# A retention block and two mixture-of-experts layers: rows of one step asked for once, scatters given out one per round, and a block of zero rows written behind other loads

## The chip, the cores and the metric

The kernel runs on one core of a Trainium2 chip. The metric is device microseconds of one execution. Five instruction streams run beside each other and wait for one another through semaphores: TensorE (PE, with its weight loads shown as PEld), VectorE (DVE), ScalarE (ACT), GpSimd (POOL) and SyncE (SP). SP computes nothing here; it issues the plain transfers. POOL issues the indirect ones (scatters of rows to places that a list of indices names).

## What is computed

The program is three stages in a row, all in float32:

```
# stage 1, for 4 batches x 8 heads, 576 positions, head size 64
scores = q @ k.T / sqrt(64)
ret    = scores * where(i >= j, gamma_h ** (i - j), 0)
x      = (ret @ v), heads side by side          # 2304 tokens x 512

# stage 2, "layer 1": 8 experts, capacity 576 rows each
e, g   = argmax(x @ w_gate), its softmax value
y[n]   = g * (relu(x[n] @ w1[e]) @ w2[e])       # 512 -> 1024 -> 512, by the token's expert

# stage 3, "layer 2": the same with other weights, only for tokens with y @ w_skip > 0
out[n] = y[n] + g2 * (relu(y[n] @ w1b[e2]) @ w2b[e2])     (else out[n] = y[n])
```

## The kernel before

**Attention.** A function `round_(u)` runs for u = 1 to 20 (`round_(0)` comes first). There are 20 units: 4 batches times 5, where four units are pairs of heads over the first 512 positions and the fifth is a tail with the last 64 positions of all heads. A round transposes the keys and queries of unit u + 1 (tiles `Tk`, `Tq`, line 187), multiplies by the states of unit u - 1 (`O`, lines 236 and 240), makes the scores of unit u (`S`, line 204), multiplies those of unit u - 1 by its values (line 246), makes the state of unit u + 1 (`kv`, line 216) and then asks for unit u + 5 (`load`). The scaled queries and values (`qp`, `vh`, function `prep`, lines 165 to 171) are made by POOL. Loads are kept in four buffers, so unit u + 4's loads wait for the buffers of unit u.

Between its parts a round has three places (`slot`) at which it takes one piece of work from a list `g.bg`. The pieces of a batch of tokens (`tokens_out(g, b)`) are: `logits`, `choose`, the rows (transposes `xps`, line 601), `step`, which computes the index of each row, and `put`. A `put` scatters T tiles of 128 rows (4 for even b, 5 for odd b) into the table `xs1` in memory: one indirect transfer for each tile, line 467. The list is `[logits, choose, rows.., step, rows.., put]` and starts for batch 0 in round 5, for batch 1 in round 11, for batch 2 in round 15; batch 3 follows after the attention.

The table of an expert's rows must hold zeros where no row is written. `clear(1)` does that for `xs1` (lines 1235 and 1238): 252 x 8 pieces of 32 bytes and 100 x 8 rows of 2080 bytes. It is issued by SP right behind the loads of unit 5. `clear(2)` does it for the table `xs2` of layer 2, late in the attention.

**Order.** In the attention the order of PE's work is written out by hand (`manual_schedule`); that of POOL, DVE, ACT and SP is chosen by the compiler's scheduler from the program's order and its own estimate of when each instruction is ready. In the layers only POOL's order is written by hand. Dependencies on the tables `xs1` and `xs2` are kept for the whole table: a read of rows waits for every scatter that stands ahead of it in the program, a scatter for every read ahead of it; scatters do not wait for each other.

**Layers.** Each layer has 9 steps (`pos` 0 to 8). A step takes one expert's rows, at most `CAPS[lay][pos]` of them (layer 2: 176, 324, 32, 240, ...), and that expert's weights in 4 units of 1 MB (`load_unit`, lines 678 and 679, five buffers). With more than 192 rows, the weights of a unit and the rows are split into a high and a low part: ACT makes `hi` (line 695), DVE `lo` (line 696), and a product is three matmuls. `gather(pos)` asks for a step's rows: four transfers of `xb` (line 649), one or two of `rows` (lines 663 and 665). `transposes` turns `xb` on DVE (line 722); with more than 192 rows ACT casts the result (`x_1h`, line 724) and DVE makes the rest (`x_1l`, line 725). `s1` is the first product of a step (`h`, lines 749, 754 to 756), `s2` the second (`y`, lines 814, 817 to 819). The step is cut in eight parts f = 0 to 7, two for each unit; `s1` runs one part ahead of `s2`. At f = 7 a step also runs `s1` part 0 of the next step. After a step, `post1` or `post2` turn the result (`yr`, line 845) and scatter it (line 467 into `xs2`, line 895 into the output).

**The line that asks twice.** In `Layer.run`, f counts the parts and u = base + 4 pos + f // 2 the units. Layer 2's first unit is 36 = 4 * NST:

```
if f == (0 if u == 4 * NST else 4) and (nx is not self or pos == 0):
    nx.gather(np_)
```

In layer 2's step 0, u is 36 at f = 0 and 1, 37 at f = 2 and 3, and 38 at f = 4 and 5. So the condition holds at f = 0 (u is 36) and at f = 4 as well (u is 38, and f is 4): the rows of layer 2's step 1 are asked for twice, into two sets of tiles, and what follows uses the second.

Of the kernel before, what the change touches and what calls it, by code (L numbers as in the profile page):

```python
# [29 lines left out]
NST = 9  # L30
# [16 lines left out]
LA = 3  # L47
# [58 lines left out]
def attention(g, hooks):  # L106
# [14 lines left out]
    def load(u):  # L121
        s = st[u] = K()
        b, p = s.b, s.p = u // 5, u % 5
        if tail(u):
            s.raw = g.ld.tile([128, 3, 2, 2, DH], F32, tag="t", name=f"t{b}", bufs=2)
            for i, x in enumerate((k, q, v)):
                for j in range(2):
                    nc.sync.dma_start(out=s.raw[64 * j:64 * j + 64, i].rearrange("p a h d -> p (a h) d"),
                                      in_=x[b, 4 * j:4 * j + 4, 512:576].rearrange("h p d -> p h d"))
            return  # L130
        hs = slice(2 * p, 2 * p + 2)
        s.q = g.ld.tile([128, 2, 4, DH], F32, tag="q", name=f"q{u}")
        s.k = g.ld.tile([128, 4, 2, DH], F32, tag="k", name=f"k{u}")
        s.v = g.ld.tile([128, 4, 2, DH], F32, tag="v", name=f"v{u}")
        dq = lambda: nc.sync.dma_start(out=s.q, in_=q[b, hs, 0:512].rearrange("h (p r) d -> p h r d", r=4))

        def pair(x, d):
            for hh in range(2):
                nc.sync.dma_start(out=d[:, :, hh], in_=x[b, 2 * p + hh, 0:512].rearrange("(t p) d -> p t d", p=128))

        part = lambda c0, c1: nc.sync.dma_start(out=g.tab[:, c0:c1], in_=g.ia["tab"][:, c0:c1])
        if u:
            dq()
            pair(k, s.k)
        else:
            pair(k, s.k)
            part(0, TAB0)
            dq()
        pair(v, s.v)
        if u == 0:  # L150
            part(TAB0, TAB1)
        elif u == 2:
            part(TAB1, g.tab.shape[1])
            g.small_loads()
        elif u == 5:
            g.clear(1)

    def prep(u):
# [113 lines left out]
    def round_(u):  # L272
        if u:
            slot()
        if u + 1 < NU:
            if u:
                prep(u + 1)
            transposes(u + 1, 0)
            if u:
                slot()  # L280
            transposes(u + 1, 1)
        if u:
            inter(u - 1)
            slot()
        if u < NU:
            scores(u)
        if u:
            pv(u - 1)
        if u + 1 < NU and not tail(u + 1):
            state(u + 1)  # L290
        if u + ahead < NU:
            load(u + ahead)
        if u:
            g.bg += hooks.get(u - 1, [])

# [273 lines left out]
def tokens_out(g, b):  # L569

    nc = g.nc
    n0 = 9 * (b // 2) + (4 if b % 2 else 0)
    T = 5 if b % 2 else 4
    s = K()

    def logits():
        s.l4 = g.rt1.tile([128, 640], F32, tag="l4", name=f"l4_{b}", bufs=1)
        logits4(g, g.xT[b], g.wg1, [512] if T == 4 else [320, 320], s.l4, f"L4_{b}_")

    def choose():  # L580
        L = g.rt1.tile([128, T, NL], F32, tag="L1", name=f"L1_{b}")
        token_logits(g, s.l4, T, L, f"Lt{b}_")
        s.xr = g.xr.tile([128, T, RW], F32, tag="xr", name=f"xr{b}")
        nc.gpsimd.tensor_copy(s.xr[:, :, TOK], g.tid1[:, n0:n0 + T])
        nc.gpsimd.memset(s.xr[:, :, VAL + 1:], 0.0)
        s.gen = g.r1.add(n0, T, L, f"r{b}", s.xr, late=b > 1)
        next(s.gen)

    def step():
        next(s.gen, None)  # L590

    def put():
        for t in range(T):
            g.r1.put(n0 + t, s.xr[:, t])
        g.r1.note(n0, T, s.xr)

    def row(t):
        n = n0 + t
        ps = misc(g, f"xps{n}")
        for c in range(4):  # L600
            nc.tensor.transpose(ps[:, 128 * c:128 * c + 128], g.xT[b][:, c, 128 * t:128 * t + 128], g.ident)
        nc.scalar.copy(stored(s.xr[:, t, 0:D]), natural(ps))

    rows = [lambda t=t: row(t) for t in range(T)]
    if b == 3:
        return [logits, choose] + rows, lambda: (step(), put())
    if b == 1:
        return [logits, choose, rows[0], rows[1], g.r1.pick_first, rows[2], step, rows[3], rows[4], put]
    return [logits, choose, rows[0], rows[1], None, rows[2], step, rows[3], put]


def ncap(u):
# [86 lines left out]
class Layer:  # L699
# [154 lines left out]
    def run(self, hooks, inner={}):  # L854
        g, lay = self.g, self.lay
        base = 4 * NST * (lay - 1)
        for pos in range(NST):
            for f in range(8):
                u = base + 4 * pos + f // 2
                if f % 2 == 0:  # L860
                    load_units(g, u + (LA if (lay, pos) < (1, 3) else LA2 - 1 if u == 4 * NST else LA2))
                    convert_unit(g, u + 1)
                    if self.small(pos) and f in (0, 4):
                        convert_unit(g, base + 4 * pos + 4 + f // 4)
                nx, np_ = (self, pos + 1) if pos < NST - 1 else (self.next, 0)
                if nx is not None:
                    if f == (0 if u == 4 * NST else 4) and (nx is not self or pos == 0):
                        nx.gather(np_)
                    for p in self.fetched(pos, f):
                        self.gather(p)  # L870
                    if nx is not self or pos == 0:
                        if f == 6:
                            nx.transposes(np_, [0, 1])
                            nx.transposes(np_, [2, 3])
                    elif f in (2, 4):
                        nx.transposes(np_, [f - 2, f - 1])
                for i in range(f + 1, f + 2 + (4 if self.small(pos) else self.token_major(pos))):
                    if i < 8:
                        self.s1(pos, i)
                    elif nx is not None and i < 9 + self.token_major(pos) and f > 4:  # L880
                        nx.s1(np_, i - 8)
                if f == 7 and nx is not None and nx.small(np_):
                    nx.s1(np_, 2)
                self.s2(pos, f)
                if (pos, f) in inner:
                    inner[pos, f]()
            self.evac(pos)
            self.post(pos)
            if pos in hooks:
                hooks[pos]()  # L890
# [284 lines left out]
def build(nc, tc, ia, oa, off, stage=99):  # L1175
    g = K()
    g.nc, g.tc, g.ia, g.oa = nc, tc, ia, oa
    g.wts, g.reg, g.xT = {}, {}, {}
    g.bg, g.scat = [], []
    with ExitStack() as ctx:  # L1180
        cp = g.cp = ctx.enter_context(tc.tile_pool(name="cp", bufs=1))
        dr = ctx.enter_context(tc.tile_pool(name="dr", bufs=1, space=DRAM))
# [65 lines left out]
        with ExitStack() as ac:  # L1248
            g.xb = ac.enter_context(tc.tile_pool(name="ge", bufs=1))
            g.ld = ac.enter_context(tc.tile_pool(name="ld", bufs=4))  # L1250
            g.wk = ac.enter_context(tc.tile_pool(name="wk", bufs=2))
            g.xt = ac.enter_context(tc.tile_pool(name="xt", bufs=2))
            ap = ac.enter_context(tc.tile_pool(name="ap", bufs=1))
            g.psT = ac.enter_context(tc.tile_pool(name="psT", bufs=1, space=PSUM))
            g.psS = ac.enter_context(tc.tile_pool(name="psS", bufs=2, space=PSUM))
            g.psO = ac.enter_context(tc.tile_pool(name="psO", bufs=1, space=PSUM))
            g.misc = ac.enter_context(tc.tile_pool(name="psX", bufs=2, space=PSUM))
            g.xtail = ap.tile([128, 4, DH], F32, name="xtail")
            e = Layer(g, 1, None)
            g.st0 = e.st  # L1260

            def loads():
                for u in range(LA):
                    load_unit(g, u)

            g.st3 = [ap.tile([128, 3, 128], F32, name=f"st3_{i}") for i in range(2)]
            g.st4 = [ap.tile([128, 4, 128], F32, name=f"st4_{i}") for i in range(2)]
            for x in g.st3 + g.st4:
                nc.gpsimd.memset(x, 0.0)
            attention(g, {  # L1270
                2: [small_prep],
                3: tokens_out(g, 0),
                9: tokens_out(g, 1) + [loads],
                13: tokens_out(g, 2) + [lambda: e.gather(0)],
                16: [lambda: clear(2)] + [lambda c=c: e.transposes(0, [c, c + 1]) for c in (0, 2)],
            })
            thunks, g.step3 = tokens_out(g, 3)
            with tc.manual_schedule(engines={mybir.EngineType.PE}):
                for fn in g.bg + thunks:
                    fn()  # L1280
        g.rt = mc.enter_context(tc.tile_pool(name="rt2", bufs=1))
        g.xb = mc.enter_context(tc.tile_pool(name="xb", bufs=3))
# [32 lines left out]
```

## Time and profile before

| | us |
|---|---|
| runs | 582.13 median of 3 (580.64 to 586.38) |
| the profiled execution, as a run | 578.59 |
| its span, from the first to the last instruction | 576.7 |
| PE's last product of the attention | 121 |
| PE's first product of layer 1's step 1 | 145 |
| PE's first product of layer 2's step 0 | 363 |
| PE's first product of layer 2's step 1 | 407 |

The page of the profile, its first two parts:

```
span 576.7 us, 12343 instructions
## 1 busy us (share of the span) xinstructions
PE 522.2 (91%) x4437; PEld 489.1 (85%) x4437; DVE 289.3 (50%) x881; ACT 218.9 (38%) x417; POOL 147.5 (26%) x225
## 2 busy tenths in 40 slices
PE   6959898999999999999999999980799599999994
DMA  8778889777999657575857555099597965879920
```

One digit is a slice of 14.4 us, in tenths of busy time. PE is busy in nine tenths of the span, so what is left to win is in the few slices with a lower digit: those of the first 40 us, and 28 to 32 (390 to 475 us).

### The profile page before, as it was taken

How to read it: one execution, taken by the hardware profiler on the slowest of the kernel's cores; microseconds unless marked ns; L12 is line 12 of the kernel's file. 1: busy time of each engine (PE TensorE's matmuls, PEld its weight loads, DVE VectorE, ACT ScalarE, POOL GpSimd, SP SyncE). 2: the span in 40 equal slices, each digit the busy share in tenths (PEclk: the TensorE clock that was granted, in tenths of full speed). 3: DMA queues.
4: the chain of work that ended last, by engine and by line, in shares of the span. 5: the costliest groups of instructions: out<-in, count | busy, mean ns of one | idle time of the engine just before them, and what ended most of it. 6: DMA issues, size and time to landing. Idle time of an engine off the chain costs nothing.

```text
span 576.7 us, 12343 instructions
## 1 busy us (share of the span) xinstructions
PE 522.2 (91%) x4437; PEld 489.1 (85%) x4437; DVE 289.3 (50%) x881; ACT 218.9 (38%) x417; POOL 147.5 (26%) x225
## 2 busy tenths in 40 slices
PE   6959898999999999999999999980799599999994
PEld 5949786979899999999999999980798489999994
DVE  4726594732467576766677765531446332211211
ACT  2224352441355464756566564321234131111110
POOL 4324736504304050414241505121002101101111
PEclk7889998999999999999999999995799799999998
DMA  8778889777999657575857555099597965879920
GB/s 194 150 196 197 243 207 320 247 235 240 291 316 291 203 176 204 173 203 160 218 178 201 181 182 155 13 258 271 142 291 197 368 198 176 256 251 296 301 83 26
DMA packets 140654, 122.35 MB, mean 212 GB/s; under 512 B 54995, under 2 KB 114131, under 8 KB 140583
## 3 DMA queue, kind: packets, MB, share of 16 engines
q1 hardware_dynamic: 134711, 108.73, 67.2%
q0 software_dynamic: 5872, 12.74, 5.9%
q8 instruction: 37, 0.61, 0.4%
q14 instruction: 34, 0.28, 0.2%
HBM read 103.21 MB, written 23.09 MB: 219 GB/s over the span
## 4 chain that ended last, share of the span: by engine, by line
PE 50%; issue 32%; DMA 6%; POOL 5%; SPq 3%; DVE 2%; ACT 1%; POOLq 0%; ACTq 0%; DVEq 0%
PE h L756 5%; PE h L755 5%; PE y L817 5%; PE h L754 5%; PE y L819 5%; PE y L818 5%; POOL out L895 3%; PE S L204 3%; DMA k<-k 2%; PE O L246 2%; DMA xs<-xr,idx 2%; PE h L749 2%; PE y L814 2%; PE Tk L187 2%; DMA r<-w1a 2%
## 5 line engine op out<-in xcount | busy, mean ns | idle before, releaser
L696 DVE TENSOR_TENSOR lo<-r,hi 128x1024 fp32r<-128x1024 f32 x72 | 87.9, 1224 | 56.3 <-ACT hi L695 54.3
L695 ACT CAST hi<-r 128x1024 fp32r<-128x1024 f32 x72 | 75.4, 1048 | 45.4 <-PE y L818 18.3
L814 PE MATMUL y<-hh,r 128*128 128x176 f32 (+4 forms) x512 | 81.8, 303 | 0.2 <-ACT hh L751 0.2
L817 PE MATMUL y<-hh,hi 128*128 128x316 f32 (+7 forms) x256 | 76.4, 300 | 0.0
L819 PE MATMUL y<-hh,lo 128*128 128x316 f32 (+7 forms) x256 | 76.0, 297 | 0.0
L818 PE MATMUL y<-hl,hi 128*128 128x316 f32 (+7 forms) x256 | 75.8, 297 | 0.0
L814 PEld LDWEIGHTS y<-hh,r 128*128 128x128 f32 x512 | 74.3, 190 | 0.5 <-ACT hh L751 0.4
L751 ACT ACTIVATE hh<-h 128x176 f32<-128x176 f32 (+4 forms) x64 | 19.6, 307 | 112.4 <-PE h L749 112.4
L895 POOL DMA_INDIRECT out<-o,oi x17 | 16.4, 968 | 165.8 <-DVE o L965 163.0
L759 ACT ACTIVATE hh<-h 128x316 fp32r<-128x316 f32 (+8 forms) x72 | 29.1, 404 | 75.9 <-PE h L756 75.8
L818 PEld LDWEIGHTS y<-hl,hi 128*128 128x128 f32 x256 | 48.3, 189 | 0.0
L819 PEld LDWEIGHTS y<-hh,lo 128*128 128x128 f32 x256 | 48.2, 188 | 0.0
L817 PEld LDWEIGHTS y<-hh,hi 128*128 128x128 f32 x256 | 48.1, 188 | 0.1
L760 DVE SCALAR_TENSOR_TENSOR hl<-h,hh 128x316 fp32r<-128x316 f32 (+8 forms) x72 | 32.2, 448 | 31.4 <-ACT hh L759 31.3
L833 DVE COPY yt<-y 128x176 f32<-128x176 f32 (+12 forms) x32 | 12.1, 384 | 59.5 <-ACT yt L835 38.4
L467 POOL DMA_INDIRECT xs<-x2s,idx x24 | 28.2, 1175 | 43.6 <-ACT hh L759 15.1
L207 DVE TENSOR_TENSOR P<-S,tab 128x512 f32<-128x512 f32 (+1 forms) x40 | 23.6, 632 | 18.0 <-PE S L204 17.8
L895 POOL DMA_INDIRECT out<-x2r,si x24 | 27.2, 1135 | 7.3 <-issue 6.1
L754 PE MATMUL h<-x_1h,hi 128*128 128x324 f32 x32 | 10.7, 341 | 19.3 <-ACT x_1h L724 19.3
L756 PE MATMUL h<-x_3h,lo 128*128 128x296 f32 (+1 forms) x64 | 19.1, 299 | 6.6 <-DVE lo L696 6.6
L754 PEld LDWEIGHTS h<-x_1h,hi 128*128 128x128 f32 x32 | 6.6, 209 | 19.6 <-ACT x_1h L724 19.6
L845 PE MATMUL yr<-ident,yt 128*128 128x128 f32 (+11 forms) x156 | 23.0, 279 | 0.0
(571 smaller groups left out, 1203.9 us busy)
## 6 DMA issues: line engine op xcount, KB each, us to landing
r<-w1a SPq DMA_DIRECT2D x36, 512.0 KB
r<-w2a SPq DMA_DIRECT2D x36, 512.0 KB
r<-w1b SPq DMA_DIRECT2D x36, 512.0 KB
r<-w2b SPq DMA_DIRECT2D x36, 512.0 KB
k<-k SPq DMA_DIRECT2D x32, 128.0 KB
q<-q SPq DMA_DIRECT2D x16, 256.0 KB
v<-v SPq DMA_DIRECT2D x32, 128.0 KB
xs<-zero SPq DMA_DIRECT2D x1, 2080.0 KB
```

Of the source, the lines that this page charges most:

```text
L695: nc.scalar.copy(hi, raw)
L696: nc.vector.tensor_sub(lo, raw, hi.bitcast(F32))
L754: nc.tensor.matmul(ps, w.hi1[:, c, fc], s.xh[:, c, 0:C], start=(c == 0), stop=False)
L755: nc.tensor.matmul(ps, w.hi1[:, c, fc], s.xl[:, c, 0:C], start=False, stop=False)
L756: nc.tensor.matmul(ps, w.lo1[:, c, fc], s.xh[:, c, 0:C], start=False, stop=(c == 3))
L759: nc.scalar.activation(s.hh[f], ps, AF.Relu)
L760: nc.vector.scalar_tensor_tensor(out=s.hl[f], in0=ps, scalar=0.0, in1=s.hh[f].bitcast(F32), op0=ALU.max, op1=ALU.subtract)
L814: nc.tensor.matmul(y, w.r2[:, f % 2, dc], s.hh[f], start=a, stop=o)
L817: nc.tensor.matmul(y, wh, s.hh[f], start=a, stop=False)
L818: nc.tensor.matmul(y, wh, s.hl[f], start=False, stop=False)
L819: nc.tensor.matmul(y, wl, s.hh[f], start=False, stop=o)
L895: r = g.nc.gpsimd.indirect_dma_start(out=g.oa["out"][:, :].rearrange("n (b d) -> (n b) d", b=parts), out_offset=IndirectOffsetOnAxis(ap=id ...
```

## The change

Three edits. First, the condition that asks for rows goes by the step (layer 2, pos 0) and no longer by the unit, so that layer 2's step 1 is gathered once, at f = 0. (The same form in the `load_units` line selects the same place as before.) Second, `put` issues one scatter; a list `g.puts` holds them, and each round from the seventh on takes one from it at its end, after `load`. The gather of layer 1's step 0 rows goes on the same list, behind batch 1's scatters and ahead of batch 2's, where it used to stand behind batch 2's; what is left on the list when the rounds end (three of batch 2's scatters) is issued then, ahead of the transposes of layer 1's step 0 and of batch 3's work. Third, `clear(1)` stands behind the loads of unit 10 and no longer behind those of unit 5.

```diff
@@ load, in attention
-        elif u == 5:
+        elif u == 10:
             g.clear(1)
@@ round_, at its end
         if u + ahead < NU:
             load(u + ahead)
+        if g.puts and u > 6:
+            g.puts.pop(0)()
         if u:
             g.bg += hooks.get(u - 1, [])
@@ tokens_out
-    def put():
-        for t in range(T):
-            g.r1.put(n0 + t, s.xr[:, t])
-        g.r1.note(n0, T, s.xr)
+    def put(t):
+        g.r1.put(n0 + t, s.xr[:, t])
+        if t == T - 1:
+            g.r1.note(n0, T, s.xr)
+
+    def puts():
+        g.puts += [lambda t=t: put(t) for t in range(T)]
...
     if b == 3:
-        return [logits, choose] + rows, lambda: (step(), put())
+        return [logits, choose] + rows, lambda: (step(), [put(t) for t in range(T)])
     if b == 1:
-        return [logits, choose, rows[0], rows[1], g.r1.pick_first, rows[2], step, rows[3], rows[4], put]
-    return [logits, choose, rows[0], rows[1], None, rows[2], step, rows[3], put]
+        return [logits, choose, rows[0], rows[1], g.r1.pick_first, rows[2], step, rows[3], rows[4], puts, lambda: g.puts.append(g.first)]
+    return [logits, choose, rows[0], rows[1], None, rows[2], step, rows[3], puts]
@@ Layer.run
-                    load_units(g, u + (LA if (lay, pos) < (1, 3) else LA2 - 1 if u == 4 * NST else LA2))
+                    load_units(g, u + (LA if (lay, pos) < (1, 3) else LA2 - 1 if (lay, pos, f) == (2, 0, 0) else LA2))
...
-                    if f == (0 if u == 4 * NST else 4) and (nx is not self or pos == 0):
+                    if f == (0 if (lay, pos) == (2, 0) else 4) and (nx is not self or pos == 0):
                         nx.gather(np_)
@@ build
-    g.bg, g.scat = [], []
+    g.bg, g.scat, g.puts = [], [], []
...
-            g.st0 = e.st
+            g.st0, g.first = e.st, lambda: e.gather(0)
...
-                13: tokens_out(g, 2) + [lambda: e.gather(0)],
-                16: [lambda: clear(2)] + [lambda c=c: e.transposes(0, [c, c + 1]) for c in (0, 2)],
+                13: tokens_out(g, 2),
+                16: [lambda: clear(2)],
             })
             thunks, g.step3 = tokens_out(g, 3)
             with tc.manual_schedule(engines={mybir.EngineType.PE}):
-                for fn in g.bg + thunks:
+                turns = [lambda c=c: e.transposes(0, [c, c + 1]) for c in (0, 2)]
+                for fn in g.bg + g.puts + turns + thunks:
                     fn()
```

## Rows read from the trace of the kernel before

**Rows 1.** Waits of PE over the span: total, times, longest (us).
```profile
PE h L754 <- ACT x_1h L724: 19.3, 1, 19.3
PE Tk L187 <- DMA k<-k: 9.0, 3, 7.0
```
**Rows 2.** Timeline of SP's issues, layer 2's step 0: start, us, line, transfer.
```profile
379.92 1.90 SPq L649 DMA_DIRECT2D xb<-xs  x4
...
383.25 0.40 SPq L678 DMA_DIRECT2D r<-w1b  x1
...
389.52 5.19 SPq L649 DMA_DIRECT2D xb<-xs  x4
```
**Rows 3.** Timeline, layer 2's steps 0 and 1; brackets: idle before, who ended it.
```profile
386.09 0.34 DVE L833 COPY yt<-y 128x176 f32<-128x176 f32 x1 [4.57 <-PE y L814]
...
390.51 1.04 ACT L695 CAST hi<-r 128x1024 fp32r<-128x1024 f32 x1 [3.82 <-DMA r<-w1b]
...
392.96 1.23 DVE L696 TENSOR_TENSOR lo<-r,hi 128x1024 fp32r<-128x1024 f32 x1
...
405.14 1.70 DVE L722 STREAM_TRANSPOSE x_1f<-xb 128x704 f32<-128x704 f32 x2 [10.95 <-DMA xb<-xs]
406.09 1.57 ACT L724 CAST x_1h<-x_1f 128x704 fp32r<-128x704 f32 x2 [13.15 <-DVE x_1f L722]
...
406.92 0.91 PE L754 MATMUL h<-x_1h,hi 128*128 128x324 f32 x2 [19.29 <-ACT x_1h L724]
...
412.74 0.31 PE L817 MATMUL y<-hh,hi 128*128 128x324 f32 x1
```
**Rows 4.** One stretch: busy us of PE, PEld, DVE, ACT, POOL; clock, DMA share, GB/s.
```profile
384.00:385.00 1.00, 1.00 (x9) 1.00 (x8) 0.00 (x0) 0.32 (x1) 0.00 (x0) 1.00 1.09 216
```
**Rows 5.** Timelines of SP, POOL and PE around the block of zeros.
```profile
24.01 3.86 SPq L1238 DMA_DIRECT2D xs<-zero  x1
27.97 0.99 SPq L135 DMA_DIRECT2D q<-q  x1
...
40.48 1.04 POOL L169 TENSOR_TENSOR qp<-q,tab 128x512 f32<-128x512 f32 x1 [9.99 <-DMA q<-q]
...
41.41 1.08 PE L187 MATMUL Tk<-ident,k 128*128 128x128 f32 x4 [6.96 <-DMA k<-k]
```
**Rows 6.** Stretches of the attention, columns as in rows 4.
```profile
34.00:36.00 2.00, 0.44 (x5) 0.00 (x0) 1.11 (x5) 0.59 (x1) 0.00 (x0) 1.00 0.73 195
...
42.00:44.00 2.00, 2.00 (x12) 2.00 (x11) 0.55 (x3) 0.59 (x1) 1.67 (x2) 0.50 1.02 240
```
**Rows 7.** Timelines of POOL and PE at the scatters of batches 0 and 1.
```profile
66.78 0.69 PE L216 MATMUL kv<-vh,k 128*64 128x64 f32 x16 [1.50 <-POOL vh L171]
...
86.43 1.04 POOL L467 DMA_INDIRECT xs<-xr,idx  x1 [0.81 <-DVE st L224]
...
92.59 1.06 POOL L171 TENSOR_TENSOR vh<-v,tab 128x512 f32<-128x512 f32 x1
...
93.71 1.12 PE L216 MATMUL kv<-vh,k 128*64 128x64 f32 x16 [2.68 <-POOL vh L171]
...
98.65 0.19 POOL L584 COPY xr<-tab 128x5 f32<-128x5 f32 x1 [4.00 <-DMA xs<-xr,idx]
```
**Rows 8.** Timelines of SP, PE, DVE and POOL at the attention's end.
```profile
115.73 1.91 SPq L649 DMA_DIRECT2D xb<-xs  x4
...
119.38 0.90 DVE L722 STREAM_TRANSPOSE x_0h<-xb 128x320 f32<-128x320 f32 x2 [0.91 <-DMA xb<-xs]
...
120.43 0.66 PE L246 MATMUL O<-P,vh 128*64 128x128 f32 x8
...
125.07 0.27 POOL L356 TENSOR_TENSOR r3sh<-L,r3mx 128x40 f32<-128x40 f32 x1 [10.47 <-DVE r3mx L354]
...
144.94 1.46 PE L749 MATMUL h<-x_1h,r 128*128 128x176 f32 x8 [1.17 <-DVE x_1h L722]
```
**Rows 9.** Timeline of DVE, layer 2's step 3.
```profile
453.71 0.16 DVE L960 TENSOR_TENSOR oi<-of,rows 128x2 int32<-128x2 f32 x1 [8.03 <-DMA out<-o,oi]
```

## Prediction

> **What bounds the kernel now.** I read the page first: PE is busy in nine tenths of the span, so an edit pays only where PE stands still, or by what it lets slip into such a place. The list of PE's waits names those places [rows 1]: one wait of 19.3 us at the first product of layer 2's step 1, for `x_1h`, and 9.0 us in the attention for keys, 7.0 of them in one piece. Then I read the timeline around each, engine by engine. Around 390 us it shows which transfer `x_1h` came from [rows 2, 3]; around 24 to 41 us what stands ahead of the late keys [rows 5, 6]; at the scatters, POOL between PE and its operands [rows 7]; at the end of the attention, how little room a later gather has [rows 8].
>
> **Edit 1, rows asked for once.** SP asks for the rows at 379.92 us and again at 389.52 [rows 2]. Between the two stand the weights of three units, and the second set of rows comes behind them: DVE can turn `xb` only at 405.14, ACT casts at 406.09, PE goes on at 406.92 after 19.29 us of nothing [rows 3]. Nobody waits for the first set, so the trace doesn't show when it lands. Two bounds: not later than 390.5, when the next transfer behind it (unit 41, asked for at 383.25) is being converted [rows 2, 3]; not before about 384, since four pieces of 176 KB at 216 GB/s [rows 4] take 3.3 us from their start near 381. The nearest like it, layer 1's step 0, went from issue at 115.73 to turned at 119.38, 3.65 us for 160 rows [rows 8]; 352 rows of 2 KB against 160 (0.72 MB against 0.33) make it 1.8 us more at that rate, 5.5 in all: 385.4. DVE stands idle for 4.57 us until 386.09 [rows 3], so the two turns (0.85 us each) and casts (0.8 each) can follow at once, with `x_1l` behind. PE's work on step 0 ends at 406.92 - 19.29 = 387.6, and I take 388.5 for the first product of step 1. That is 406.9 - 388.5 = 18.4 us.
>
> Two things lie behind that. PE comes back from its pause at half clock (0.50, the 1.2 GHz level, as after the other pause [rows 6]): from its start at 406.92 to the first `s2` at 412.74 are 5.8 us [rows 3] for two parts of `s1`, which at full clock take 2 x 12 products of about 0.15 us (0.31 shown, overlapped by half) = 3.6. So 2 us more come back. Against it, the third part of `s1` needs unit 41, whose `lo` is ready at 392.96 + 1.23 = 394.2 at the latest [rows 3]; PE would be there at about 388.5 + 5.4 = 393.9, with DVE now crowded by `x_1l`, `post2` and `lo` at once: I take off 1.5. Sum: 18.4 + 2 - 1.5 = **19 us**. What is late next is unit 41 and its conversion; from there a part costs PE 3.6 us, a unit 7.2, and a unit's 1.05 MB takes 4.4 us to load at 240 GB/s [rows 6], so the loads keep ahead. Bounds: up to 21 with no crowding. If DVE keeps its present order, `lo` of unit 41 before the turn, the turn starts at 394.2 and PE at 406.92 - (405.14 - 394.2) = 396: 11 us. A saved 1.4 MB of transfers itself counts for nothing beyond this: they only fill the same pause.
>
> A second pause stays where it is: DVE stands 8.03 us for a scatter of step 1's results [rows 9]; all that leads to it moves together.
>
> **Edit 3, zeros behind unit 10.** SP issues the zeros at 24.01 and the queries of unit 6 at 27.97 [rows 5]. These land at 40.48, 12.5 us later, and PE waits 6.96 us for the keys until 41.41, then runs at half clock (0.50 in 42 to 44 us [rows 6]) for some 4.4 us where 2.5 would do. Without the zeros unit 6's keys come some 10 us earlier, ahead of PE, which wants them at 41.41 - 6.96 = 34.45: 7.0 + 1.9 = 8.9 us. The cover for the moved zeros is the depth of the loads. Round 5 starts with the keys of unit 6, round 9 ends with the state of unit 10, 66.78 + 0.69 [rows 7]: 26.1 us, less 1.9 of slow clock and 1.5 of waiting, is 4.5 us a round. So PE wants unit 11 at 34.45 + 5 x 4.5 = 57. Units 6 to 10 (3.5 MB at 240 GB/s, 15 us) start about where the zeros did, at 24 to 26 us; the zeros add 11 (by unit 6's delay), unit 11 another 3.5: in at 54 to 56. That is close, so up to 3 us of waiting. The zeros also meet a new partner: the first scatter of batch 0 writes the same table, so it must wait until they are in (50 to 52 us), stands in POOL's queue from round 7's end (34.45 + 3 x 4.5 = 48, somewhat later with batch 0's pieces) and holds the `qp` and `vh` of the next rounds. That is 0 to 6 us, partly the same time. I take -2.5 for both: **6.4 us**, bounds 0 (the pause only moves) to 8.9.
>
> The Trainium skill, in "DMA: Bandwidth & Descriptors", section "Why a DMA increments its semaphore by 16 and not by 1", says that a transfer spreads over the largest number up to 16 that divides the slowest dimension, 100 partitions over 10 engines. The rows of zeros have 100, and the trace agrees with a transfer on part of the engines: a DMA share of 0.73 while PE stands waiting [rows 6]. By this rule later loads wait for those ten engines wherever the zeros stand; edit 3 would give 0 and the time be 562, where my reading of the rows says 556.
>
> **Edit 2, one scatter a round.** Batch 1's five scatters hold POOL from 86.43 to 92.59, 1.23 us each, and `vh` behind them lets PE wait 2.68 us [rows 7], with some 1.2 us more at a low clock after it. Spread over rounds 14 to 18 each fits into POOL's idle time. At batch 0 the wait of PE is 1.50 us [rows 7]; there POOL stood for a landed scatter, which stays, so I count nothing. **3.9 us**, bounds 0 (POOL's order is the scheduler's; it may still line them up) to 5.4.
>
> The same list moves the gather of layer 1's step 0, and this may cost. Before, it was issued at 115.73, turned at 119.38, and PE left the attention at 121.1 [rows 8], so it was hidden by 1 us. Now it stands behind the scatter of round 18, two rounds ahead of the attention's end, say 6 us with the short last one. That scatter takes 1.2 us and up to 6 to land (batch 1's last one ended at 92.59 and POOL saw it landed at 98.65 [rows 7]), the gather 3.65: ready up to 5 us after the end. Batch 3's products can cover a part. Batch 2's scatters now wait for this gather's read and then need 4 x 1.23 = 4.9 us on POOL, until up to 10 us after the end. If batch 3's `r3sh`, 4.0 us after the end before (125.07 against 121.1 [rows 8]), stands behind them, batch 3's indices and scatters are up to 6 us late. These set the gather of layer 1's step 1, which PE already waits for by 1.17 us [rows 8]. So 0 to 8 us; I take **-3**.
>
> **Sum.** 19 + 6.4 + 3.9 - 3 = 26.3 us. Layer 1 lies between the edits with PE at ten tenths, so what is won ahead of it is carried through. The profiled execution took 578.6 us as a run (span 576.7); 552.3 after. The runs' median is 582.13, so 555.8: I say **556**.
>
> **Rivals.**
> - *DVE's order stays, or the rows land with unit 41.* Edit 1 gives 11 to 13 us: some 19 in all, 563. For it: the scheduler, not the program, orders DVE. Against: with one gather the turn is ready before the conversion. Chance 0.13.
> - *The pause moves with the zeros.* Units 11 to 13 wait for the same 11 us, their lead is used up, and PE waits for keys near 57 us as it did at 34; edit 3 gives 0, and what edit 2 gives goes to the new order at layer 1's start. Edit 1 alone: 563. For it: a margin of only 1 to 3 us at unit 11. Against: behind unit 11 the loads gain on PE, 3.5 us a unit against 4.5 a round. The page named above is on this side. Chance 0.17; together with the rival above 570, 0.03.
> - *All parts at their best* (21 + 8.9 + 5.4, nothing given back), or the second pause [rows 9] shrinks too: 547 or less. Chance 0.08.
> - *Nothing changes:* the step 1 products turn out held by something else at 405, as by weights of units 42 and 43 behind each other. Against it, PE waits for `x_1h` alone. If edits 2 and 3 cancel too, 578 to 582; chance 0.03.
> - *Slower:* the first scatter holds POOL until the zeros are in, and PE has no `qp`. Each us of lateness costs one; it must be over 27 us late to outweigh the rest, beyond 77 us instead of 52, and 33 us for 588. The zeros took about 11 us. Chance 0.02.
>
> **How the numbers follow.** The forecast (550 to 561) has 0.54. From 546 to 569 the range takes in the first two rivals and the edge of the third. A difference of 1% (5.8 us) is about what a measurement can tell from none: faster 0.95, same 0.03, slower 0.02.
>
> **What would show it.** Right: one set of `xb` and `rows` transfers in layer 2's step 0; PE's wait for `x_1h` under 3 us and no half clock behind it; no wait for keys at 34 us and a DMA queue that reaches the zeros near 40; POOL's scatters a round apart. Wrong: a wait for `lo` or `hi` at layer 2's step 1 as long as the old one; waits for keys or `vh` near 55 us; a wait over 5 us for `x_0h` or `x_1h` of layer 1.

## The result, and the profile after

| | before | after |
|---|---|---|
| median of the runs, same chip | 584.25 us | 564.93 us |
| profiled execution, span | 576.7 us | 560.5 us |
| ratio of the runs, 95% interval | 1 | 0.969 [0.960, 0.978] |

The change makes the kernel faster by 3.1%. Runs more than 1.5% above the fastest of their kernel are left out of all ratios, and of the times in the experiments: one of the four before (589.79 us), two of the four with edit 1 alone (571.8 and 572.8), one of four each with the even zeros (568.6) and with edits 1 and 2 and POOL by hand (574.0), and one of 1775 us. Forecast were 556 us in a range of 546 to 569: the sign and the range hold, the value is 9 us too low. To see where, cut both timelines at the same five instructions: the last product of attention (PE, `O<-P,vh`), the first product of layer 1's step 1 (`h<-x_1h`), the first `yr` of layer 2's step 0, the first product of layer 2's step 1, and the scatter with which the last step's results begin to leave (POOL, `out<-o,oi`). The lengths between them, in us:

| stretch | before | after | difference | forecast |
|---|---|---|---|---|
| A: start to the last product of attention | 120.4 | 118.9 | -1.6 | -10.3 |
| B: to layer 1, step 1 | 24.5 | 31.0 | +6.5 | +3 |
| C: to layer 2, step 0, `yr` | 241.5 | 241.7 | +0.2 | 0 |
| D: to layer 2, step 1 | 20.4 | 2.2 | -18.2 | -18.4 |
| E: to the last step's scatter | 163.1 | 160.0 | -3.1 | -0.5 |

So edit 1 did what was worked out for it, and edits 2 and 3 together lost where 7 us had been expected from them.

**D and E, edit 1.** Timelines of SP, DVE and PE in the changed kernel around layer 2's steps 0 and 1 (start, duration, engine, line, operation; in brackets the idle time before and what ended it):

```profile
385.10 1.90 SPq L654 DMA_DIRECT2D xb<-xs  x4
...
391.80 0.34 DVE L838 COPY yt<-y 128x176 f32<-128x176 f32 x1 [0.26 <-PE y L819]
392.06 1.69 DVE L727 STREAM_TRANSPOSE x_1f<-xb 128x704 f32<-128x704 f32 x2
...
393.82 0.56 PE L759 MATMUL h<-x_1h,hi 128*128 128x324 f32 x2 [1.08 <-ACT x_1h L729]
...
439.51 0.16 DVE L965 TENSOR_TENSOR oi<-of,rows 128x2 int32<-128x2 f32 x1 [0.52 <-DMA out<-o,oi]
...
461.87 0.50 PE L813 MATMUL y<-hi,hl 128*128 128x512 f32 x1 [1.03 <-DVE hl L765]
```

One set of rows is asked for, at the time of the first set before; DVE turns them with no wait for a transfer, 6.96 us after the issue, and PE's wait of 19.29 us [rows 3] is 1.08. The line of 439.51 is the second pause: 8.03 us of DVE in [rows 9], 0.52 now. In the kernel before, DVE made a `lo` right behind that pause, and PE waited for it:

```profile
455.10 0.57 PE L756 MATMUL h<-x_3h,lo 128*128 128x240 f32 x1 [6.61 <-DVE lo L696]
```

That wait is 0.66 us in the changed kernel (at 435.12). The last line of its timeline is a wait that grew instead, from 0.65 to 1.03 us; the experiments come back to it.

**A, edits 2 and 3.** PE's waits from 0 to 125 us in the changed kernel (total, times, longest in us):

```profile
PE Tk L187 <- DMA k<-k: 6.3, 3, 3.2
PE Tq L187 <- POOL qp L169: 4.3, 1, 4.3
PE kv L216 <- POOL vh L171: 2.7, 1, 2.7
```

Timelines of SP, PE and POOL for the same:

```profile
41.80 3.89 SPq L1243 DMA_DIRECT2D xs<-zero  x1
45.79 0.78 SPq L135 DMA_DIRECT2D q<-q  x1
46.67 2.04 SPq L139 DMA_DIRECT2D k<-k  x1
...
59.43 0.63 PE L187 MATMUL Tk<-ident,k 128*128 128x128 f32 x4 [3.22 <-DMA k<-k]
59.52 1.19 POOL L469 DMA_INDIRECT xs<-xr,idx  x1 [5.94 <-issue]
61.01 0.98 POOL L469 DMA_INDIRECT xs<-xr,idx  x1 [0.31 <-ACT kT L189]
62.29 0.98 POOL L469 DMA_INDIRECT xs<-xr,idx  x1 [0.30 <-issue]
63.29 1.06 POOL L169 TENSOR_TENSOR qp<-q,tab 128x512 f32<-128x512 f32 x1
64.40 1.11 PE L187 MATMUL Tq<-ident,qp 128*128 128x128 f32 x4 [4.34 <-POOL qp L169]
...
86.04 1.04 POOL L469 DMA_INDIRECT xs<-xr,idx  x1 [0.81 <-DVE st L224]
...
91.24 0.98 POOL L469 DMA_INDIRECT xs<-xr,idx  x1 [0.30 <-issue]
...
93.36 0.69 PE L216 MATMUL kv<-vh,k 128*64 128x64 f32 x16 [2.71 <-POOL vh L171]
```

The 6.96 us at 34 us [rows 5] are gone. In their place unit 11's keys, asked for behind the zeros, come 3.22 us late, and POOL stands 5.94 us in front of the first scatter; the trace names no releaser, but this scatter may not write the table before the zeros are in. Three scatters then go in a row ahead of unit 11's `qp`, and PE waits another 4.34 us. It comes back at half clock; the stretch (columns: busy time of PE, PEld, DVE, ACT, POOL; clock, DMA share, GB/s):

```profile
61.00:71.00 10.00, 6.60 (x56) 6.14 (x59) 1.29 (x2) 0.96 (x2) 7.00 (x9) 0.50 0.92 257
```

The last three lines of the timeline are batch 1: its five scatters went out in a row once more, from 86.04 to 92.22 us, and the wait behind them is 2.71 us where it was 2.68 [rows 7].

**B, layer 1's start.** Timelines of SP, DVE and PE in the changed kernel:

```profile
100.93 2.34 SPq L1243 DMA_DIRECT2D xs<-zero  x2
103.52 7.01 SPq L654 DMA_DIRECT2D xb<-xs  x4
...
126.65 0.25 PE L478 MATMUL fc<-C,onesr 128*128 128x8 f32 x1
130.34 0.15 DVE L1006 CAST flag<-ov1n 128x1 int32<-128x1 f32 x1
130.52 0.91 DVE L727 STREAM_TRANSPOSE x_0h<-xb 128x320 f32<-128x320 f32 x2
131.08 4.63 PE L754 MATMUL h<-x_0h,r 128*128 128x160 f32 x16 [4.18 <-DVE x_0h L727]
...
149.87 1.36 PE L754 MATMUL h<-x_1h,r 128*128 128x176 f32 x8
```

The gather of step 0 now goes out 12 us earlier than in [rows 8], but its turn comes 11 us later (130.52 against 119.38), with no wait for a transfer in front of it: in DVE's order it stands behind all index work of the last batch, down to the flag of line 1006. PE runs dry until 131.08; before, step 0's products filled it while that index work went on.

### The profile page after: what moved, and what is told of

It reads as the page before. It is cut to its first block, busy times and chain, and to the rows that moved or that the text cites. A ratio compares the mean times of both kernels' runs of the same rounds, so it can differ in the third digit from the quotient of the medians.

```text
span 560.5 us, 12333 instructions
## 1 busy us (share of the span) xinstructions
PE 524.3 (94%) x4437; PEld 491.7 (88%) x4437; DVE 287.5 (51%) x881; ACT 219.4 (39%) x417; POOL 149.8 (27%) x224
## 4 chain that ended last, share of the span: by engine, by line
PE 62%; issue 23%; POOL 4%; DMA 3%; DVE 3%; ACT 2%; SPq 1%; POOLq 0%; DVEq 0%; ACTq 0%
PE y L822 6%; PE h L760 6%; PE h L761 6%; PE y L824 6%; PE h L759 6%; PE y L823 6%; PE h L754 5%; PE y L819 4%; PE S L204 3%; DMA k<-k 3%; PE O L246 2%; POOL out L900 2%; PE yr L850 2%; PE xps L606 1%; PE O L240 1%
## 5 line engine op out<-in xcount | busy, mean ns | idle before, releaser
L900 POOL DMA_INDIRECT out<-o,oi x17 | 18.3, 1079 | 150.1 <-DVE o L970 147.7
L900 POOL DMA_INDIRECT out<-x2r,si x24 | 28.4, 1183 | 7.3 <-issue 5.8
L754 PE MATMUL h<-x_0h,r 128*128 128x160 f32 (+1 forms) x128 | 23.6, 331 | 4.2 <-DVE x_0h L727 4.2
L754 PEld LDWEIGHTS h<-x_0h,r 128*128 128x128 f32 x128 | 20.8, 207 | 4.7 <-DVE x_0h L727 4.3
L204 PE MATMUL S<-qT,kT 64*128 64x128 f32 x288 | 23.4, 303 | 0.0
```

The costliest lines, as they stand in the source:

```text
L204: nc.tensor.matmul(S[hh][:, c], s.kT[hp, cs], s.qT[hp, cs], start=True, stop=True)
L754: nc.tensor.matmul(ps, w.r1[:, c, fc], s.xh[:, c, 0:C], start=(c == 0), stop=(c == 3))
L900: r = g.nc.gpsimd.indirect_dma_start(out=g.oa["out"][:, :].rearrange("n (b d) -> (n b) d", b=parts), out_offset=IndirectOffsetOnAxis(ap=id ...
```

## The experiments

Each ratio is to the kernel before on the same chip. The stretches of every profiled execution, named as above:

| kernel | A | B | C | D | E | ratio, 95% interval |
|---|---|---|---|---|---|---|
| before | 120.4 | 24.5 | 241.5 | 20.4 | 163.1 | 1 |
| after | 118.9 | 31.0 | 241.7 | 2.2 | 160.0 | 0.969 [0.960, 0.978] |
| edit 1 alone | 121.4 | 24.5 | 245.4 | 2.2 | 159.1 | 0.957 (medians, two runs) |
| edits 2 and 3 | 119.3 | 30.6 | 245.8 | 20.0 | 164.6 | 1.005 [1.002, 1.009] |
| edits 1 and 3 | 124.1 | 27.2 | 244.1 | 2.2 | 160.9 | 0.969 [0.964, 0.974] |
| edits 1 and 2 | 119.9 | 28.0 | 245.8 | 2.2 | 165.2 | 0.977 [0.972, 0.982] |
| edit 1, even zeros | 118.1 | 24.5 | 245.5 | 2.2 | 164.3 | 0.958 [0.949, 0.967] |
| edits 1 and 2, POOL by hand | 117.4 | 30.7 | 244.7 | 2.2 | 164.6 | 0.968 [0.958, 0.978] |
| after, zeros of layer 2 moved | 123.1 | 27.8 | 242.7 | 2.2 | 162.6 | 0.968 [0.962, 0.974] |
| after, turn by hand | 120.1 | 25.0 | 241.5 | 2.2 | 162.4 | 0.964 [0.960, 0.968] |
| put together otherwise | 109.0 | 30.2 | 241.5 | 2.2 | 165.5 | 0.961 [0.959, 0.963] |
| after, again | 119.7 | 30.1 | 241.7 | 2.2 | 161.2 | 0.975 [0.971, 0.979] |
| put together otherwise, again | 111.5 | 30.9 | 241.4 | 2.2 | 159.8 | 0.961 [0.958, 0.964] |

Column D is the cleanest: 2.2 us in every kernel with edit 1, 20.4 and 20.0 in the two without. Two kernels were profiled twice; their two executions differ by up to 2.5 us in A, 0.9 in B and 5.7 in E, so smaller differences between rows say little.

E holds two waits that go with edit 1. The second pause is 7.7 to 8.0 us in the two kernels without the edit and at most 0.8 in the eleven with it, and PE's wait for `lo` behind it falls from 6.6 and 6.3 us to 1.0 at most. The other is PE's wait for `hl` in step 3 (line 813, in the kernel before 808): 0.5 and 0.7 us without the edit, 1.0 to 4.8 with it. DVE makes that `hl` behind the turn of step 5's rows, and the turn, in all kernels of the table but two, waits for these rows. In the kernel put together otherwise:

```profile
453.24 0.58 DVE L727 STREAM_TRANSPOSE x_5h<-xb 128x384 f32<-128x384 f32 x1 [10.82 <-DMA xb<-xs]
...
454.16 0.79 PE L813 MATMUL y<-hi,hl 128*128 128x512 f32 x1 [4.75 <-DVE hl L765]
```

E is 165.5 us with this wait of 4.75, and 159.8 in the second execution of the same kernel, where it was 1.26; in the changed kernel 160.0 with 1.03, and 161.2 again with 3.23. So E's spread goes with this wait, and the 3.1 us of the pair are what the first wait gave back, less the second. Why the rows of step 5 come sooner in one execution than in another isn't shown.

**Edit 1 alone, and all but edit 1.** To the kernel before, and the other way round to the changed one:

```diff
-                    if f == (0 if u == 4 * NST else 4) and (nx is not self or pos == 0):
+                    if f == (0 if (lay, pos) == (2, 0) else 4) and (nx is not self or pos == 0):
```

> Edit 1 alone: the kernel before with the rows of layer 2's step 1 asked for once; scatters, first gather and zeros as before. Theory (edit 1 wins about 21 us, edits 2 and 3 together lose about 5): 21 us under before, so some 5 us under the changed kernel; the attention ends at 121 us and layer 2 starts as before, PE's wait for x_1h is near 1 us. Rival (edits 2 and 3 cost nothing or win, as forecast): 16 to 19 us under before, not faster than the changed kernel.

> Edits 2 and 3 without edit 1: the changed kernel with the rows of layer 2's step 1 asked for twice again. Theory: 5 us slower than before. Rival (edits 2 and 3 win as forecast): 3 to 7 us faster than before.

Measured: 561.1 and 562.2 us against 587.1 with edit 1 alone, 25 us less where the theory had 21; 589.7 against 587.1 without it, where the theory had 5 us more. Edit 1 carries the whole gain; edits 2 and 3 together cost 0.2 to 0.9% of the kernel before, some 3 us. What they cost beside edit 1 is less sure, with two runs and a spread of 6 us in E; no run shows a gain.

**Each of the other edits beside edit 1.** The kernel before with edits 1 and 3:

```diff
-        elif u == 5:
+        elif u == 10:
             g.clear(1)
```

> Edits 1 and 3: rows asked for once, zeros behind unit 10; scatters of a batch in one piece of work and the first gather behind batch 2's, as before. Theory (the pause only moves with the zeros): within 3 us of edit 1 alone, no wait for keys at 34 us, but PE standing 7 us or more near 55 to 65 us, for keys and then for qp behind the scatters that wait for the zeros. Rival (the wait at 60 us comes of the scatters given out one by one): 6 us or more faster than edit 1 alone.

and the changed kernel with edit 3 taken back, which leaves edits 1 and 2:

> Edits 1 and 2: rows asked for once, scatters on the list, first gather on the list; zeros behind unit 5 as before. Theory (the moved gather costs at layer 1's start, the scatters stay lined up): 3 to 8 us slower than edit 1 alone, PE idle after the attention's end for x_0h, batch 1's five scatters still in a row with PE waiting 2.7 us behind them. Rival (the zeros made the late start, through the scatters): within 1 us of edit 1 alone or faster.

PE's waits until 125 us with edits 1 and 3:

```profile
PE Tq L187 <- POOL qp L169: 6.0, 1, 6.0
PE Tk L187 <- DMA k<-k: 5.6, 3, 2.3
```

With edit 1 alone the keys cost 10.1 us. The moved zeros halve that and bring 6.0 us for `qp` behind the held scatter: attention ends at 124.1 instead of 121.4 us. So edit 3 moves the pause and doesn't shorten it. With edit 2 attention ends at 119.9, 1.5 us earlier; batch 1's scatters still stand in a row (86.51 to 92.69 us), but PE waits only 0.5 us behind them and not 2.7. The times are 566.9 us with edits 1 and 3 and 571.1 with edits 1 and 2, 5 and 9 us above the two runs of edit 1 alone; the theories had at most 3, and 3 to 8.

Each of the two edits lengthens B, edit 2 by 3.5 us and edit 3 by 2.7, though edit 3 leaves the gather where it was (115.42 us). What differs is the place of step 0's turns in DVE's order. Timelines of DVE with edit 1 alone, with edits 1 and 3, and with edits 1 and 2:

```profile
119.33 0.89 DVE L722 STREAM_TRANSPOSE x_0h<-xb 128x320 f32<-128x320 f32 x2
...
128.83 0.91 DVE L722 STREAM_TRANSPOSE x_0h<-xb 128x320 f32<-128x320 f32 x2
...
125.82 0.90 DVE L727 STREAM_TRANSPOSE x_0h<-xb 128x320 f32<-128x320 f32 x2
```

The first stands ahead of the last batch's index work, the other two in the midst of it, that of the changed kernel (130.52) at its end; B is 24.5, 27.2, 28.0 and 31.0 us.

**Zeros in even pieces.** The kernel before with edit 1, and 112 whole rows of zeros for each expert instead of 100:

```diff
-CLEAR = {1: 252, 2: 128}
+CLEAR = {1: 240, 2: 128}
```

> The kernel before with edit 1 alone (its median 567.0 us, ratio 0.966), and of the zeros behind unit 5 the whole rows number 112 instead of 100 for each expert (the first 240 rows get their tails zeroed instead of 252), so that their rows divide evenly over 16 engines. Theory: the keys behind the zeros wait for the bytes ahead of them, 1.66 MB before and 1.86 MB now; PE's waits for keys stay at 9 to 11 us in sum (10.1 with edit 1 alone), the time at 567 +- 2 us. Rival: the pause is long because 100 rows fill 10 of 16 engines only; then the zeros take 10/16 of their time, the waits for keys fall to about 6.5 us in sum and the time to 563 us.

Measured: the longest wait for keys fell by more than half, and attention ended at 118.1 us instead of 121.4. The time was 563.3 us, ratio 0.958; against edit 1 alone (0.957 in two runs) the end time shows no gain, with E 5 us longer in this execution. PE's waits and the busy share of the DMA engines from 23 to 42 us (40 slices, tenths) with 100 rows, edit 1 alone:

```profile
PE Tk L187 <- DMA k<-k: 10.1, 3, 5.9
...
DMA  9999853433355789669766656966689595543699
```

and with 112 rows:

```profile
PE Tk L187 <- DMA k<-k: 5.5, 3, 2.7
...
DMA  9799844433599999999999999999977997999889
```

More bytes (1.86 MB against 1.66) go through sooner. With 100 rows the share stands near six tenths for as long as the zeros and the loads behind them run, with 112 near ten. This is the rule of the Trainium skill that the prediction cited, "DMA: Bandwidth & Descriptors", section "Why a DMA increments its semaphore by 16 and not by 1": by it 100 rows go over 10 engines and 112 over 16. The trace agrees, with six tenths of the engines' time and nearly ten, and the theory, that only bytes count, fell. The changed kernel shows the same six tenths at the zeros' new place, 41 to 60 us:

```profile
DMA  7999722224166989669767966665686855477389
```

**Zeros in eight pieces.** Edit 1, two experts' zeros behind unit 5, one each behind units 6, 7, 8, 10, 11 and 12:

```diff
-        elif u == 5:
-            g.clear(1)
+        if u in PIECE:
+            for e_ in PIECE[u]:
+                g.clear(1, slice(e_, e_ + 1))
```

> The kernel before with edit 1 alone, and the zeros cut into one piece for each expert: two pieces behind the loads of unit 5, one each behind units 6, 7, 8, 10, 11 and 12. Theory: PE's loss in the first half of attention is the one long transfer that stands ahead of one unit's keys; in pieces of about 1.1 us each it hides in the slack between loads, the waits for keys fall from 10.1 us in sum to under 4, attention ends 5 to 6 us earlier than with edit 1 alone (last product 121.4 us), the time is about 561 us (ratio 0.956). Rival: the queues have no slack until 60 us, so the bytes cost their time wherever they stand: the waits, spread over several units, keep a sum of 8 to 10 us or move to the first scatter, and the time stays at 567 us.

Its results are undefined, for a reason that stays open, so only its attention is read. PE's waits until 130 us (the lines of this kernel are two further down):

```profile
PE Tq L189 <- POOL qp L171: 5.9, 4, 4.4
PE Tk L189 <- DMA k<-k: 5.5, 4, 2.1
PE Tq L189 <- POOL qp L167: 4.1, 2, 3.1
```

The keys' wait fell to 5.5 us, not under 4. The first scatter went out at 66.00 us against 56.01 with edit 1 alone, and attention ended at 126.8 us, 5.4 later. That fits a first scatter that waits for the last piece, which is one of the rival's two cases; the trace doesn't name the wait.

**POOL's order by hand.** Edits 1 and 2, zeros behind unit 5:

```diff
-    with g.tc.manual_schedule(engines={T.PE}):
+    with g.tc.manual_schedule(engines={T.PE, T.Pool}):
         for u in range(1, NU + 1):
```

> Edits 1 and 2 with the zeros behind unit 5 as before (571.1 us, ratio 0.977, without the rest of this edit), and POOL's instructions of the rounds of attention held in the order of the program, so that one scatter of rows really follows each round's qp and vh. Theory: edit 2 gave nothing because POOL's order was the scheduler's, which put the five scatters of batch 1 in a row again; held by hand, PE's waits for qp and vh of POOL behind unit 5 fall under 1 us (1.7 there now, 2.7 in the changed kernel), and the time falls by 2 to 4 us to 567 to 569 us. Rival: a round leaves POOL no room for a scatter of 1 to 1.3 us beside qp and vh of 2 us, or the program's order itself makes POOL wait; PE's waits for POOL stay or grow, and the time is 571 us or more.

Timeline of POOL, batch 1:

```profile
89.75 1.04 POOL L469 DMA_INDIRECT xs<-xr,idx  x1 [0.16 <-ACT kT L189]
90.82 1.06 POOL L169 TENSOR_TENSOR qp<-q,tab 128x512 f32<-128x512 f32 x1
91.92 1.05 POOL L171 TENSOR_TENSOR vh<-v,tab 128x512 f32<-128x512 f32 x1
...
96.35 1.04 POOL L469 DMA_INDIRECT xs<-xr,idx  x1 [0.48 <-ACT r2sh L359]
```

Now the scatters do stand a round apart, the five from 89.75 to 109.43, and PE has no wait for POOL left in attention, which ends 2.4 us earlier than without (117.4). That is no more than two executions of one kernel differ, but the waits for POOL are gone. The end time doesn't show it (569.5 us; the intervals overlap): B grew from 28.0 to 30.7.

**Layer 2's zeros behind the gather.** The changed kernel with

```diff
-            g.st0, g.first = e.st, lambda: e.gather(0)
+            g.st0, g.first = e.st, lambda: (e.gather(0), g.clear(2))
...
-                16: [lambda: clear(2)],
```

> The changed kernel with one thing moved: the 3.7 MB of zeros for layer 2 are asked for behind the gather of layer 1's first step (as before) instead of ahead of it. Theory: the changed kernel starts layer 1 late (first product at 131.1 us instead of 121.7) because that gather queues behind these zeros, and the order on DVE and PE was made for a late gather; moved, the first product comes at 121 to 123 us, among the products of the last batch's logits and rows, layer 1's first results of yr come 5 to 7 us earlier, and the time is 558 to 560 us (ratio 0.957). Rival: the gather is late because it now stands behind batch 1's five scatters in the list, one a round, wherever the zeros are; then the first product stays past 128 us and the time at 565 us.

Timelines of PE, POOL and DVE:

```profile
114.85 0.54 PE L754 MATMUL h<-x_0h,r 128*128 128x160 f32 x2
118.06 0.94 PE L240 MATMUL O<-qT,st 128*128 128x128 f32 x6 [2.67 <-ACT xT L257]
133.61 0.99 POOL L469 DMA_INDIRECT xs<-xr,idx  x1 [5.60 <-DVE idx L457]
150.25 1.04 DVE L727 STREAM_TRANSPOSE x_1h<-xb 128x384 f32<-128x384 f32 x2
150.89 4.20 PE L754 MATMUL h<-x_1h,r 128*128 128x176 f32 x16 [1.26 <-DVE x_1h L727]
```

The first product came at 114.85 us, earlier than the theory said, and layer 1's first `yr` 7 us earlier (147.06 against 154.17), and still the time stayed at 0.968. Step 1 is what ends this stretch. It needs the rows that the last batch scatters; their indices now stood behind step 0's work, the first of these scatters went out at 133.61 us instead of 128.74, and step 1 began at 150.89; and attention, with step 0's products among its own, ended 4.2 us later (123.1). So the loss is neither in the gather's place nor in step 0's start alone: DVE and PE must do the last batch's work and step 0 side by side.

**The turn by hand.** The changed kernel, with DVE held to the program's order in the last part of attention, which puts step 0's turns ahead of the last batch's index work:

```diff
-            with tc.manual_schedule(engines={mybir.EngineType.PE}):
+            with tc.manual_schedule(engines={mybir.EngineType.PE, mybir.EngineType.DVE}):
                 turns = [lambda c=c: e.transposes(0, [c, c + 1]) for c in (0, 2)]
```

> The changed kernel with one thing moved in VectorE's order: the turns of layer 1's step 0 (x_0h) are held by hand ahead of the index work of the last batch, behind the last scores of attention, as they stood before. Theory: the changed kernel gave its gains in attention back at layer 1's start, where 31.0 us lie between the last product of attention and the first product of step 1 (24.5 before), because that turn stood behind all index work of the last batch and TensorE idled; moved, step 0's products fill TensorE again, its first product comes at 123 to 126 us instead of 131.1, step 1's first at 145 to 147 instead of 149.9, the time falls by 3 to 5 us to 560 to 562 us. Rival: step 1 sets the end of this stage and waits for the rows that the last batch scatters; its index work, now behind the turn, comes later by as much as step 0 comes earlier: step 1's first product stays at 149 to 151 us and the time at 565 us.

Timelines of DVE and PE:

```profile
119.01 0.91 DVE L727 STREAM_TRANSPOSE x_0h<-xb 128x320 f32<-128x320 f32 x2 [0.85 <-DMA xb<-xs]
...
145.12 1.46 PE L754 MATMUL h<-x_1h,r 128*128 128x176 f32 x8 [1.71 <-DVE x_1h L727]
```

B is 25.0 us, as before the change, and the time 560.0 us against 579.8 of the kernel before; the interval lies wholly under that of the changed kernel run again (on another chip, where the kernel before took 580.9 us), but overlaps that of its first measurement. For B the theory stands: 6 us of the changed kernel hang on DVE's order here, in which two turns of 0.5 us now stand 11.5 us earlier. The edit holds all of DVE's order in this part, so some small instructions moved with them.

**Put together otherwise.** The changed kernel with the zeros even and behind unit 5, POOL by hand, layer 2's zeros behind the gather and the turns by hand:

> The changed kernel put together otherwise: zeros behind unit 5 as before, with 112 whole rows for each expert instead of 100; POOL's order in the rounds held by hand, so that the scatters really go one a round; the zeros of layer 2 behind the gather of layer 1's step 0; that step's turns by hand ahead of the last batch's index work. Theory: attention ends at 114 to 116 us (118.1 with the even zeros and edit 1, 2.4 us less with POOL by hand), step 1 begins 24.5 to 26 us behind it at 139 to 142 us, the time is 559 to 562 us (ratio 0.953). Rival: in POOL's order by hand the scatters of the last two batches, nine in a row of 1.3 us, stand behind one another; step 1's rows wait for the last of them, its first product stays at 145 to 148 us as with POOL by hand before (148.1), and the time is 565 to 568 us.

> The changed kernel itself, beside the version put together otherwise on the same chip. Theory: ratio to the kernel before 0.966 to 0.972, with 31 us between the last product of attention and the first of layer 1's step 1 again. Rival: the 31 us were of one execution; then they are nearer to 25, and the ratio is 0.963 or lower, as with the turns held ahead.

> The version put together otherwise (even zeros behind unit 5, POOL by hand, layer 2's zeros behind the gather, turns by hand), again, beside the changed kernel on one chip. Theory: ratio to the kernel before 0.959 to 0.963, about 4 us under the changed kernel. Rival: its earlier attention is not in the end time; then it is within 2 us of the changed kernel.

It took 557.9 us against 579.8, and, beside the changed kernel on one chip, 557.6 against 566.0 (580.9 before): 1.5% faster than the changed kernel, which here gave 0.975 where 0.966 to 0.972 was expected. It isn't shown to be faster than edit 1 alone (0.961 against 0.957 in two runs). Attention ends at 109.0 and 111.5 us, earlier than forecast from the parts. But B is 30 us again, for another reason. Timeline of PE in the second execution:

```profile
111.49 0.66 PE L246 MATMUL O<-P,vh 128*64 128x128 f32 x8
...
117.83 0.90 PE L754 MATMUL h<-x_0h,r 128*128 128x160 f32 x2 [3.38 <-DVE x_0h L727]
```

Attention now ends before step 0's rows are there: with one scatter a round the gather behind them is asked for only at 113.64 us, and DVE waits 7.74 us for its rows. By the 24.5 us of B before, some 6 us could still be had here; that is an estimate that no run tried. One execution of its second measurement took 1775 us, three times the others; there is no trace of it, and its cause stays open.

## Why the prediction was right and wrong

- **Edit 1: right.** First product of step 1 forecast 18.4 us earlier, 18.2 measured in D, and D is 2.2 us in all kernels with the edit. Two details were not: the half clock came all the same (PE waits only 1.08 us, yet the clock from 394 to 400 us is 0.72 and the first `s2` comes at 399.74, 5.9 us behind the first product, as before), so the "2 us more" did not come back; and the second pause did not "stay where it is". It went, and with it 6.6 us of PE's waiting, of which 3.1 us are left in E where 0.5 was forecast. This gain came by luck: without it the time would have been 567 to 568 us, close to the end of the range.
- **Edit 3: the term of 6.4 us was not there.** Beside edit 1 alone the moved zeros end attention 2.7 us later (124.1 against 121.4), beside edits 1 and 2 they end it 1.0 us earlier (118.9 against 119.9; 0.2 in the second execution), which is within what two executions of one kernel differ by. The step that failed is "the zeros add 11, ... in at 54 to 56", and with it "until they are in (50 to 52 us)". PE wanted unit 11 at 56.2 us, as forecast (57), but its keys were in at 59.4, and the first scatter went at 59.5. The zeros and the loads behind them run on part of the engines, so the queue is at six tenths all that time, and the depth of the loads, worked out from 240 GB/s, was not there. For the zeros' old place the even rows show it; at the new place they weren't tried, and it is argued from the same six tenths. The prediction had the rule and the share of 0.73, and put it among the rivals: "the pause moves with the zeros", 563 us. That rival is what happened in A.
- **Edit 2: the term of 3.9 us took the lower bound it named.** "It may still line them up" is what the changed kernel did: the waits at batch 1 are 2.68 and 2.71 us. Held by hand, the scatters gave 2.4 us in attention where 3.9 had been put, and took away all of PE's waits for POOL there. Beside edit 1 little of the term was left to win: with edit 1 alone PE's waits for `vh` come to 0.4 us in attention, where they were 4.2 before.
- **The moved gather: the cost of 3 us was 3.5, by another mechanism, and edit 3 added as much again.** B grew by 3.5 us with edits 1 and 2, by 2.7 with edits 1 and 3, where the gather stands as before, and by 6.5 with all three. The forecast had the rows late and POOL busy with batch 2's scatters ahead of `r3sh`. `r3sh` ran at 122.58, ahead of them, 2.5 us earlier than before; what was late was the turn, by DVE's order. Its rows had landed: nothing stood between it and the instruction ahead of it at 130.52, and with the turns by hand the rows were there at 119.01, asked for at 104.78. The step that failed is the assumption that a turn runs when its data are there, and the moved zeros' cost at layer 1's start was put at nothing without a reason.
- **Sum.** 26.3 us forecast, 16.2 in the profiled pair: 18.2 + 1.6 - 6.5 - 0.2 + 3.1.

Left open: why the scheduler put the turn so late. Moving layer 2's zeros behind the gather also moved the turn forward, which speaks for the time at which it expects the rows, but it isn't shown.

## What to carry to other kernels

When an edit moves a transfer or an issue, read the new order on every engine around it, not only the moved instruction: here two turns of 0.5 us took back 6 us. A large transfer whose slowest dimension doesn't divide over all DMA engines costs the loads behind it more than its bytes say, and a few rows more can make it shorter. What one wait of 19 us on one transfer gives back could be forecast to within 0.2 us; what the same edit did to the order of the engines 50 us later could not, nor the gains from removing several small waits that follow one another.

## What the runs showed of the hardware

- A transfer of more bytes freed the queue sooner: zeros of 1.86 MB, 112 rows for each of 8 experts, against 1.66 MB, 100 rows for each, brought the longest wait for keys from 5.9 to 2.7 us and attention's end from 121.4 to 118.1 us.
- The zeros of the first rows' tails, 32 bytes a row, 63 KB in all, move at 19 to 33 GB/s for some 2 us, behind unit 5 as behind unit 10; the three lines of the DMA share above show it as the runs of twos, threes and fours.
- The same layer 1 (stretch C) took 241.4 to 241.7 us in some of the comparisons and 242.7 to 245.8 in others; the kernels of one comparison ran on one chip. With edit 1 alone, ACT began one cast of weights at 330.69 us after 1.79 us of idleness, PE waited 1.6 us behind it, and at a clock of 0.94 that step took 29.5 us against 25.9 in the changed kernel. Profiles from different chips are therefore compared here by stretch and not by their ends.
